# Busy matmuls in a TensorE gap and an earlier last gather, at the layer ends of a DMA-bound decode kernel

## The chip, the cores and the metric

One core of one Trainium2 chip. The metric is the device time of one execution in microseconds (us); the spread between executions of one kernel here is 1 to 3 us of some 1985. The core's engines are TensorE (matrix products), VectorE, ScalarE and SyncE (which issues the transfers here); DMA engines move the data from HBM, the chip's large memory, into the core.

## The reference

Four layers, A, B, A, B, each a residual attention block for one token over a cached context of 8192 positions, 32 heads of 192:

```python
# x: [1, 1, 640] bf16; k_cache, v_cache: [1, 32, 8192, 192]; wq: [640, 6144]; wo: [6144, 640]
def _A_ref(x, k_cache, v_cache, wq, wo):        # _B_ref is the same with its own arrays
    q = (x @ wq).reshape(B, Sq, Hq, Dh).transpose(0, 2, 1, 3)
    scores = jnp.einsum("bhqd,bhkd->bhqk", q, k) * (Dh ** -0.5)
    p = _softmax(scores, axis=-1)
    o = jnp.einsum("bhqk,bhkd->bhqd", p, v)
    return o.transpose(0, 2, 1, 3).reshape(B, Sq, Hq * Dh) @ wo
...
x = x + _A_ref(_layernorm(x), ...)              # then B, A, B
```

Every layer works on about 200 MB of K and V; with the weights, and less what two layers leave on the core for the later ones, 848 MB must come in from HBM. There is little arithmetic.

## The kernel before

Heads go in 16 pairs. Per pair, VectorE multiplies K by the query, TensorE sums the products through an identity matrix into the bank S, a softmax follows, TensorE multiplies the probabilities with V into the bank O ("values"), and a "gather" picks the right blocks out of O on VectorE (8 steps, 2 for the last pair) and moves them on with small matmuls into TB. After every 5 pairs "columns" turns the collected row into columns (`oT`), and "project" multiplies it with the 15 blocks of a part of wo, one matmul with one moving column per block and output group. The order of a layer's end is in a list of steps; every engine works the list in its order:

```python
# ... a part of the loop over layers l; p is the last pair, 15; NB = [0, 5, 0, 5]
steps.append(("e", l, p - 1))                                     # gather of pair 14
steps += [("v", l, p, 0), ("wc", l, 2)] if NB[l] else [("wc", l, 2), ("v", l, p, 0)]
steps += [("wo", l, 2), ("v", l, p, 1)]                           # wo: first 10 of 15 blocks
if NB[l]:
    plan.append(("vq", l))                                        # last quarter of pair 15's V
    both(("wob", l))                                              # the last NB[l] = 5 wo blocks
steps.append(("e", l, p))                                         # gather of pair 15
both(("wol", l))                                                  # pair 15's own rows of wo
```

`plan` is the order of these transfers, all issued by SyncE on one queue. At the end of a B layer it is: first half of pair 15's V, the third quarter, the last quarter (`vq`), the last five wo blocks (`wob`), pair 15's rows of wo (`wol`). `wol` lands in a row buffer, so its issue must wait for "columns" (`wc`); in layer 1 the first wq rows of layer 2 are issued right behind it.

## Time and profile before

| | before |
|---|---|
| time at first, 3 runs | 1984.95 us (1984.85 to 1985.31) |
| span of the profiled run, granted clock | 1984.0 us, 0.776 |
| DMA | 848.36 MB, 428 GB/s over the span |
| landing of `wob` in layer 3 | 1977.70 us |
| from there to the end of the last matmul | 3.29 us |
| from there to the end of the span | 6.3 us (2.4 of them the store of the result) |

The table's landings are in the trace's records of when each transfer's semaphore was updated: 16 updates, as many as the page counts DMA engines, and the transfer has landed with the last. The granted clock is the mean share of its full clock that TensorE was given; the trace's records of it hold 1.00 and 0.50 alone, in stretches that are multiples of 3.413 us (all 202 of the profile before but the last, in which the record ends). The lines of a profile's timeline in this document read: start, duration, engine, line of the kernel, operation, tiles (written <- read), shapes and count; in brackets the idle time before and what ended it. PE stands for TensorE's matmuls, DVE for VectorE, ACT for ScalarE. The lines of a chain of waits have the start, the duration and what was waited for. To read the table: the DMA stream fills the span (428 GB/s as a mean, 427 to 438 in 37 of its 40 slices), so there are two kinds of place where time can be won, at a stretch where the stream runs dry, and in the tail after its last landing.

### The profile page before, as it was taken

The numbers are of one execution on the slowest core, as the hardware profiler recorded it, in microseconds if no ns is written. First come the engines' busy times: TensorE is split into PE (matmuls) and PEld (weight loads), VectorE is DVE, ScalarE is ACT, GpSimd is POOL, SyncE is SP. The second block draws the span as 40 slices with busy tenths as digits, with TensorE's granted clock in tenths as the row PEclk, the third lists the DMA queues.
The fourth block names the chain that finished last, engine by engine and source line by source line (L and its number), as shares of the span: only waits on it lengthen the run. The fifth ranks groups of instructions, "written<-read, shape, count | busy, mean of one in ns | idle before, by whom it ended". The sixth has DMA issues, their size and how long they took to land.

```text
span 1984.0 us, 13908 instructions
## 1 busy us (share of the span) xinstructions
PE 1273.4 (64%) x8310; PEld 150.1 (8%) x3266; DVE 1200.7 (61%) x1371; ACT 139.5 (7%) x461; POOL 4.5 (0%) x22
## 2 busy tenths in 40 slices
PE   3567567566466666665775665675676766656657
PEld 0001001000200100100020010010002001001001
DVE  3566467467166656556745565665664775665665
ACT  0000000000000000000010000000000000000000
POOL 0000000000000000000000000000000000000000
PEclk9787777777587787777876777878886887777777
DMA  9999999999999999999999999999999999999998
GB/s 412 438 430 431 431 437 429 431 430 431 433 435 431 432 429 436 430 431 432 427 388 433 430 430 430 432 430 430 431 431 427 435 432 434 430 432 432 432 431 353
DMA packets 26926, 849.25 MB, mean 428 GB/s; under 512 B 3184, under 2 KB 3184, under 8 KB 3952
## 3 DMA queue, kind: packets, MB, share of 16 engines
q1 hardware_dynamic: 26720, 848.38, 99.5%
q8 instruction: 45, 0.74, 0.2%
q14 instruction: 17, 0.14, 0.0%
q10 hardware_dynamic: 144, 0.00, 0.0%
HBM read 848.36 MB, written 0.00 MB: 428 GB/s over the span
## 4 chain that ended last, share of the span: by engine, by line
DMA 68%; DVE 15%; PE 15%; ACT 1%; issue 0%; SPq 0%
DMA pool<-in_B_k_cache_dram 27%; DMA pool<-in_A_v_cache_dram 20%; DMA pool<-in_A_k_cache_dram 14%; DVE pool L543 13%; PE S L58 6%; PE OY L58 5%; DMA pool<-in_B_v_cache_dram 4%; PE OY L620 3%; DMA pool<-in_B_wo_dram 2%; ACT p_sb L580 1%; DVE acc L639 1%; DMA pool<-in_A_wq_dram 1%; DVE s_sb L565 1%; PE OY L513 0%; PE S L556 0%
## 5 line engine op out<-in xcount | busy, mean ns | idle before, releaser
L543 DVE TENSOR_TENSOR pool<-pool,q_sb 128x3072 bf16<-128x3072 bf16 x512 | 861.2, 1753 | 241.5 <-DMA pool<-in_B_k_cache_dram 144.0
L58 PE MATMUL S<-pool,ident 128*128 128x512 bf16 x2944 | 789.1, 425 | 20.3 <-DVE pool L543 19.0
L650 PE MATMUL TB<-acc,small 128*1 128x192 f32 x240 | 82.1, 493 | 219.1 <-DVE acc L639 219.1
L556 PE MATMUL S<-pool,ident 128*128 128x512 bf16 x128 | 62.9, 491 | 213.6 <-DVE pool L543 213.6
L58 PE MATMUL OY<-pool,p_sb 128*16 128x512 bf16 x1920 | 197.0, 485 | 0.0
L638 DVE TENSOR_SCALAR acc<-OY,small 128x192 f32<-128x192 f32 x64 | 26.7, 418 | 274.2 <-PE OY L58 246.2
L620 PE MATMUL OY<-pool,p_sb 128*16 128x512 bf16 (+1 forms) x1216 | 147.5, 497 | 62.7 <-DMA pool<-in_A_v_cache_dram 56.4
L639 DVE SCALAR_TENSOR_TENSOR acc<-OY,small,acc 128x192 f32<-128x192 f32 x424 | 177.1, 418 | 14.9
L565 DVE TENSOR_REDUCE s_sb<-S 128x64 f32<-128x512 f32 x128 | 88.1, 688 | 69.4 <-PE S L58 69.4
L502 ACT ACTIVATE q_sb<-QM 128x192 bf16<-128x192 f32 x60 | 19.9, 331 | 954.8 <-PE QM L496 954.8
L661 ACT ACTIVATE rows<-TB,small 1x192 bf16<-1x192 f32 x120 | 43.2, 406 | 585.1 <-PE TB L650 585.1
L634 DVE RECIPROCAL small<-TB 1x2 f32<-1x2 f32 x64 | 11.2, 175 | 96.7 <-PE TB L595 75.2
L580 ACT ACTIVATE p_sb<-s_sb,small 64x128 bf16<-64x128 f32 x128 | 55.7, 435 | 161.9 <-DVE small L574 161.1
L556 PEld LDWEIGHTS S<-pool,ident 128*128 128x128 bf16 x128 | 13.0, 101 | 686.2 <-DVE pool L543 636.4
L595 PE MATMUL TB<-small,ones 128*1 128x2 f32 x120 | 11.4, 165 | 74.1 <-ACT p_sb L580 74.1
L620 PEld LDWEIGHTS OY<-pool,p_sb 128*16 128x16 bf16 (+1 forms) x1216 | 39.3, 107 | 203.6 <-issue 133.5
L570 PE MATMUL QM<-ident,m_bf 128*64 128x64 bf16 x128 | 14.1, 217 | 54.4 <-DVE m_bf L567 53.8
L650 PEld LDWEIGHTS TB<-acc,small 128*1 128x1 f32 x240 | 19.7, 101 | 311.4 <-DVE acc L639 283.9
L513 PE MATMUL OY<-oT,pool 128*128 128x1 bf16 x900 | 38.2, 178 | 3.5 <-ACT oT L528 2.8
L513 PEld LDWEIGHTS OY<-oT,pool 128*128 128x128 bf16 x900 | 37.1, 131 | 7.0 <-ACT oT L528 3.6
L574 DVE TENSOR_REDUCE small<-QM 128x1 f32<-128x64 f32 x64 | 14.4, 225 | 36.1 <-PE QM L570 36.1
L496 PEld LDWEIGHTS QM<-rows,one_b 1*64 1x64 bf16 x120 | 6.2, 100 | 350.7 <-issue 344.8
(59 smaller groups left out, 186.1 us busy)
## 6 DMA issues: line engine op xcount, KB each, us to landing
pool<-in_B_k_cache_dram SPq DMA_DIRECT2D x28, 6144.0 KB, 38.1
pool<-in_B_v_cache_dram SPq DMA_DIRECT2D x28, 6144.0 KB, 34.2
pool<-in_A_v_cache_dram SPq DMA_DIRECT2D x27, 6144.0 KB, 27.6
pool<-in_A_k_cache_dram SPq DMA_DIRECT2D x34, 3072.0 KB, 20.4
pool<-in_A_k_cache_dram SPq DMA_DIRECT2D x14, 6144.0 KB, 36.8
pool<-in_A_v_cache_dram SPq DMA_DIRECT2D x10, 3072.0 KB, 14.3
pool<-in_B_k_cache_dram SPq DMA_DIRECT2D x8, 3072.0 KB, 22.7
pool<-in_A_wo_dram SPq DMA_DIRECT2D x6, 2400.0 KB, 21.4
```

The source lines that it names most:

```text
L58: return t.add_instruction(mybir.InstMatmult(name=t.bass.get_next_instruction_name(), engine=mybir.EngineType.PE, ins=[t.lower_ap(rhs), t. ...
L502: lambda a: a.activation(q_sb[i][:], QM[:, 0:DH], ACT.Copy), e, last["q"][i], bank=QMu)
L513: e = PE.op(lambda t, i=i, c=c, f=y_first[0], fin=n[0] == "wol" and i == k - 1: t.matmul(YB[:, c:c + 1], lhsT=t3[:, i, c:D:DC], rhs=o[:, i ...
L543: e = DV.op(lambda v, d0=d0: v.tensor_tensor(k3[:, :, d0:d0 + QD], kin[:, :, d0:d0 + QD], q_sb[qi][:, d0:d0 + QD].unsqueeze(1).broadcast_t ...
L556: t.matmul(S[:, :], lhsT=ident[:], rhs=k3[:, :, d0:d0 + R], start=True, stop=fin) if d0 == 0 else
L565: lambda v, u=u: v.tensor_reduce(s[:, u * JU:(u + 1) * JU], SP_[u][:].rearrange("p (j r) -> p j r", r=R), AX.X, ALU.add), ev_S[p, u], last ...
L580: ev_p[p] = AC.op(lambda a, h=h, r=r: a.activation(p_sb[par][r, :, h], s[r, :], ACT.Exp, bias=negm[par][r, 0:1], accum_out=l_col[par][r, h ...
L620: t.matmul(o, lhsT=x, rhs=y, start=f, stop=fin) if c == 0 else
L638: v.tensor_scalar(acc[:], O[:, 0:DH], pick[:, 0:1], None, ALU.mult) if i == 0 else
L639: v.scalar_tensor_tensor(out=acc[:], in0=O[:, i * DH:(i + 1) * DH], scalar=pick[:, i:i + 1], in1=acc[:], op0=ALU.mult, op1=ALU.add)), e if ...
L650: e = PE.op(lambda t, h=h: t.matmul(TB[96:97, C_O + h * DH:C_O + (h + 1) * DH], lhsT=half[:, h:h + 1], rhs=acc[:], start=True, stop=True), ...
L661: last["TO"] = last["row_written"] = AC.op(lambda a, h=h: a.activation(orow[:, o0 + h * DH:o0 + (h + 1) * DH], TB[96:97, C_O + h * DH:C_O ...
```

## The change

It is meant to do two things at the ends of layers 1 and 3 (the two B layers). While VectorE picks pair 14 out of the bank O, TensorE idles for 4.15 us, and its granted clock is 0.50 from 1966.99 on in layer 3 and from 1001.02 on in layer 1 (1.00 before); 16 matmuls of the identity on itself, written to a bank that nobody reads, are to keep it up. And the gather of pair 15 is put ahead of the last wo part, so that ScalarE's step behind the gather lies beside that part.

```diff
@@ -262,13 +262,15 @@
-            steps.append(("e", l, p - 1))
+            steps += [("busy", l, 16), ("e", l, p - 1)] if NB[l] else [("e", l, p - 1)]
             steps += [("v", l, p, 0), ("wc", l, 2)] if NB[l] else [("wc", l, 2), ("v", l, p, 0)]
             steps += [("wo", l, 2), ("v", l, p, 1)]
             if NB[l]:
                 plan.append(("vq", l))
+                steps.append(("e", l, p))
                 both(("wob", l))
-            steps.append(("e", l, p))
+            else:
+                steps.append(("e", l, p))
             both(("wol", l))
@@ -412,6 +414,16 @@
+        def busy(n):
+
+            PE.wait(ev_const, last["S"][0])
+            for i in range(n):
+                PE.op(lambda t, i=i: (
+                    t.matmul(SP_[0][:, :], lhsT=ident[:], rhs=ident[:].unsqueeze(1).broadcast_to([P, 4, P]), start=True, stop=True)
+                    if i == 0 else
+                    matmul_held(t, SP_[0][:, :], ident[:], ident[:].unsqueeze(1).broadcast_to([P, 4, P]), True, True)),
+                    signal=False, bank=Su[0])
@@ -672,6 +684,8 @@
+                elif n[0] == "busy":
+                    busy(n[2])
```

## The prediction

> **What bounds the kernel now.** I read the page first, for the engines and the DMA rows. They say that the sixteen DMA engines are never idle for long while TensorE and VectorE are busy some 60% each.
>
> ```profile
> PE 1273.4 (64%) x8310; PEld 150.1 (8%) x3266; DVE 1200.7 (61%) x1371; ACT 139.5 (7%) x461; POOL 4.5 (0%) x22
> ...
> DMA  9999999999999999999999999999999999999998
> GB/s 412 438 430 431 431 437 429 431 430 431 433 435 431 432 429 436 430 431 432 427 388 433 430 430 430 432 430 430 431 431 427 435 432 434 430 432 432 432 431 353
> ```
>
> The stream runs at some 430 GB/s everywhere but in slice 20 (from layer 1 into layer 2, 388) and in the last slice (353). 848.36 MB at 430 GB/s are 1973 us of the 1984, so all starts, ends and gaps together are worth about 11 us. The change touches just these two places, the ends of layers 1 and 3. So next I read the chain of waits there.
>
> ```profile
> 987.05 15.80 DMA pool<-in_B_v_cache_dram
> 1002.89 2.73 PE OY L620 x32
> ...
> 1007.03 13.21 DMA pool<-in_A_wq_dram
> ...
> 1937.57 40.13 DMA pool<-in_B_wo_dram
> 1977.74 1.16 PE OY L513 x25
> 1978.90 0.99 PE TB L646 x12
> 1980.23 0.77 PE OY L513 x15
> ```
>
> The reader is to see that the end of the kernel hangs on a transfer, the last part of wo, which lands at 1977.70; after it come 25 matmuls, the last pair's gather, and 15 matmuls. In layer 1 the chain goes through the first half of pair 15's values, then by the issue at 1007.03 to the landing of layer 2's first wq rows at 1020.24. Then the timeline of the last 25 us:
>
> ```profile
> 1962.13 0.22 PE L570 MATMUL QM<-ident,m_bf 128*64 128x64 bf16 x2
> ...
> 1963.31 3.14 DVE L639 SCALAR_TENSOR_TENSOR acc<-OY,small,acc 128x192 f32<-128x192 f32 x7
> ...
> 1966.50 0.99 PE L650 MATMUL TB<-acc,small 128*1 128x192 f32 x4 [4.15 <-DVE acc L639]
> ...
> 1968.70 2.73 PE L620 MATMUL OY<-pool,p_sb 128*4 128x384 bf16 x32
> ...
> 1977.59 0.42 DVE L638 TENSOR_SCALAR acc<-OY,small 128x192 f32<-128x192 f32 x1 [4.66 <-PE OY L620]
> ```
>
> TensorE idles 4.15 us while VectorE picks pair 14; the 32 value matmuls after it take 2.73 us, eight groups of four at 0.32 us, that is 384 columns at 1.2 per ns. The view by windows shows the clock as granted: 1.00 until 1967.0, 0.50 from there to the end. In layer 1 the gap is 4.15 us too and the clock 0.50 from 1001.0 to 1024.9.
>
> [...] the records of the clock hold only 1.00 and 0.50, in stretches of multiples of 3.413 us. I laid that grid over the trace. [...] The one-column matmuls of the wo part do not count: 0.86 of a window of them left it at 0.50. [...]
>
> **The change part by part.** (1) It adds 16 matmuls of 128x512 on the identity per B layer, 32 in all. At full clock, which the gap starts in at both places, one takes 0.216 us (12 value matmuls of 512 columns in four column groups take 0.65, so 0.217 a group), 16 take 3.46. They run from 1962.35 to 1965.8 (layer 3) and 995.99 to 999.45 (layer 1); the gather of pair 14 that follows needs TensorE at 1966.49 and 1000.14. So they fit in the gap with 0.7 us to spare and cost nothing.
>
> (2) What they buy. In layer 3, any window ending between 1965.8 and 1970.4 then holds at least 1.4 us of wide work (busy matmuls, gather 0.81, values), so the first half of the values of pair 15 should run at full clock: 8 groups of 0.163 and 0.15 of tail, 1.45 us instead of 2.73: 1.28 us saved, and 0.18 on the gather's matmuls (0.81, as in layer 1, for 0.99). In layer 1 the values start at 1002.89, bound by their landing, with 3.4 us since the last busy matmul; about a third of the positions of the window would lose the clock before them. When it holds, 1.28 us are saved there. After that come 3.2 us of one-column matmuls, which don't count, so by the second half of the values the clock is half again.
>
> (3) Where the gain goes. In layer 3 the second half of the values would start at 1973.35 instead of 1974.80, but its second quarter lands at 1975.77 (the trace's records of landings), and layer 1 shows 1.48 us from that restart to the end of the values at half clock (1010.25 to 1011.73). So they end at 1977.30 instead of 1977.53: 0.23 us of 1.46 are left. The pick on VectorE takes 0.06 + 0.87, to 1978.23.
>
> (4) The order. Before, from the landing of wo at 1977.70: wo 1.16, gather 1.04 overlapped by 0.07, ScalarE with its waits 0.36, wol 0.76: the last matmul ends at 1980.99. After, TensorE must wait for the pick: gather 1978.27 to 1979.31, wo 1.10 to 1980.41, wol 0.70 to 1981.1, with ScalarE beside wo. Hiding 0.36 costs an idle wait of 0.5. Sum: +0.1 us. If the values' second half ran at full clock, the pick would end 0.65 earlier and the sum would be about -0.5.
>
> (5) Layer 1: the same working, with the values' end unchanged at 1011.73, gives +0.1 us to the layer's end, which has slack: VectorE starts layer 2's products at 1018.57 while TensorE waits for wq until 1020.24. What could gain is the issue of that wq, 1.28 us earlier. The DMA rate had sunk to 232 and 247 GB/s at 1006 to 1008. But the landings say something else: 1006.54, 1010.20, 1012.14, 1013.32, 1020.24; their steps of 3.66, 1.94, 1.18 and 6.92 us are their bytes (1536, 800, 480, 2880 KB) at 430 GB/s. [...] So the landing at 1020.24 should hardly move: 0 to -0.6 us (the 0.6 if I am wrong and the mean rate counts: 1.28 us times 0.45 idle share).
>
> Total: +0.1 in layer 3, -0.3 in layer 1 as the middle of its two readings: -0.2 us, 1984.75. I lean a little further, to 1984.6, because the clock's phase can also help the second half of the values.
>
> **The rivals.** First: the warm clock carries through to the end, values, gather and wol all faster, and the order pays its full 0.36 + 1.04: about -1.5 us, with 0.6 of layer 1 some -2, 1983. For it: the whole tail from 1967.0 is at 0.50. Against it: the wo part between doesn't count, and transfers gate the tail. Second: the busy matmuls get in the way. Had the clock been at half there, they would take 6.8 us and hold the gather up by 2.7 us in each layer, of which the DMA backlog hides most: up to +3 us, 1988. Against it: dense work precedes the gap in both places and the clock is 1.00 there. Third: wo behind the gather frees its slot 1.5 us later in layer 1, and the wq rows for that slot are issued at 1014.9 instead of 1013.4; [...] I expect 0, at worst +0.5.
>
> **Range and chances.** The three runs of before spread 0.46 us. With the free window phase I take -1.4 to +1.0 around 1984.9 as the eight in ten: 1983.5 to 1985.9. Two per cent are 40 us, more than all gaps together on the fast side; only an accident could reach it: 1% on either side.
>
> **What would show it.** Right: 32 more S matmuls of 0.22 us; the idle time before L650 down from 4.15 to 0.7 us in layer 3; the first half of pair 15's values at 1.45 us, the second at 2.7 or stretched by its landing; L646 ahead of the 25 wo matmuls; the wo part's landing still some 6 us before the end, with the tail after it within 0.3 us of before. Wrong: a granted clock of 1.00 at the last values, or layer 2's first wq landing more than 0.6 us earlier, would mean a gain over 1 us; busy matmuls of 0.43 us would mean a loss.

That 1.4 us of wide matmuls in a window keep the clock up, in (2), and with it the third of the window's positions that would lose it, were the author's estimate. It came from two windows of the profile before: one with S matmuls for 1.26 us of its 3.41 (from 1673.45) was followed by a granted clock of 0.50, one with 1.39 (from 1731.47) by 1.00. That the one-column matmuls do not count is read from such windows too (2.95 us of them from 332.01 at 0.50, then 0.50 again). That nothing is won in (5) rests on the steps between the landings alone.

## The result

The change's median is 1985.45 us (1984.82 to 1987.35, 6 runs), that of the kernel before in the same rounds and the first ones 1985.51 us (1984.85 to 1986.53, 6 runs). The ratio is 1.0002 with a 95% interval of 0.9989 to 1.0015: the same. (A ratio here is the mean time of one kernel's fast runs over that of the other's, so it is not quite the ratio of the medians quoted.) A later trial of five rounds gave 0.9999. The time lies inside the forecast range, but that range of 2.4 us is about as wide as the runs scatter. The gain of 0.35 us against 1984.95 that was forecast did not show: the time came out 0.85 us above the forecast 1984.6, and 0.56 us of that is the kernel before itself, whose median went from 1984.95 to 1985.51 with three more runs. The interval is some 2.6 us to either side, so the times cannot tell a gain of 0.35 us from none; the traces must.

From the page of the profile after, the span, the busy time of the engines and the DMA rate by slices: 32 matmuls more, 8 us more of busy TensorE, the same two weak slices.

```profile
span 1983.5 us, 13942 instructions
...
PE 1281.3 (65%) x8342; PEld 149.7 (8%) x3268; DVE 1200.4 (61%) x1371; ACT 139.5 (7%) x461; POOL 4.4 (0%) x22
...
GB/s 412 435 434 429 430 435 432 432 429 430 434 432 436 430 429 432 432 434 430 424 402 438 425 430 430 432 431 430 433 431 428 434 430 434 431 434 433 430 432 350
```

The timeline of TensorE at the end of layer 3, after (lines lie 12 further down than before):

```profile
1961.92 0.39 PE L422 MATMUL S<-ident 128*128 128x512 bf16 x1
...
1962.14 3.40 PE L58 MATMUL S<-ident 128*128 128x512 bf16 x15
...
1966.13 0.81 PE L662 MATMUL TB<-acc,small 128*1 128x192 f32 x4 [0.59 <-DVE acc L651]
...
1968.06 1.47 PE L632 MATMUL OY<-pool,p_sb 128*4 128x384 bf16 x32
...
1972.90 1.45 PE L632 MATMUL OY<-pool,p_sb 128*4 128x384 bf16 x16
...
1974.82 1.45 PE L632 MATMUL OY<-pool,p_sb 128*4 128x384 bf16 x16 [0.46 <-DMA pool<-in_B_v_cache_dram]
```

The busy matmuls do what they were put in for: they fill the gap down to 0.59 us, the gather's matmuls take 0.81 instead of 0.99 us and the first half of pair 15's values 1.47 instead of 2.73. But the second half now stops in its middle for 0.46 us until the last quarter of its data has landed. Before, it ran through without a stop:

```profile
1974.80 2.73 PE L620 MATMUL OY<-pool,p_sb 128*4 128x384 bf16 x32
```

(Its quarter landed at 1975.77, and four groups of 0.32 us from 1974.80 on take until some 1976.1.) The view by windows of 3.413 us, the unit of the clock's records (stretch and its length; then busy time and count of PE, its weight loads, DVE, ACT and GpSimd; then the granted clock, the DMA share and rate), shows the clock that the second half got:

```profile
1965.30:1968.71 3.41, 1.92 (x27) 0.87 (x29) 0.74 (x2) 0.72 (x2) 0.00 (x0) 1.00 0.97 411
1968.71:1972.12 3.41, 3.13 (x71) 2.58 (x61) 0.17 (x1) 0.19 (x1) 0.00 (x0) 1.00 1.01 402
1972.12:1975.54 3.42, 2.96 (x50) 1.52 (x52) 0.00 (x0) 0.00 (x0) 0.00 (x0) 0.50 0.69 281
```

In the middle window TensorE is busy for 3.13 us of 3.41, but only 0.82 of that are values; the rest is columns and wo with one moving column each. The next window has 0.50, and the second half's groups take as long as before.

The chain of waits that ended last, after:

```profile
1937.51 37.26 DMA pool<-in_B_v_cache_dram
...
1974.82 1.48 PE OY L632 x15
...
1976.32 0.43 DVE acc L650
...
1976.78 0.43 DVE acc L651
...
1977.25 1.04 PE TB L658 x12
1978.29 1.71 PE OY L525 x40
```

Before, it hung on `wob`; now it hangs on the last quarter of V, landing at 1974.77, and goes through VectorE's pick and the gather into all 40 matmuls of the wo parts. `wob` itself lands at 1976.71, and TensorE waits for the pick until 1977.25. From that landing to the end of the last matmul (1979.98) are 3.27 us, against 3.29 before. That it is the last quarter that counts can be read across traces: in the five profiles of kernels that end layer 3 as the change does (the change twice, e5_delay6, e6_delay16, e7_warm2), the last matmul ends 5.21 us after that quarter's landing, while `wob` lands anything from 1.90 to 2.31 us after it. In this one profile everything is 1.0 us earlier by the landing of `wob`, but that is not the change: the change's second profile has it at 1978.02. 0.4 us of it are there before layer 2 begins, the other 0.6 come after; which part the phase of the clock's window has in that isn't shown.

In layer 1, the chain after reads:

```profile
1002.51 2.55 PE OY L632 x32
...
1006.46 13.40 DMA pool<-in_A_wq_dram
```

Here the granted clock of this execution fell to 0.50 at 1002.74, just after the values began, and they took 2.55 us. The first wq of layer 2 lands at 1019.85, 17.39 us after the first half of pair 15's V (1002.47); before it was 17.39 us too (1002.85 to 1020.24). The landing records show why the mean rate misleads here. The updates of one transfer have drifted apart: of the 16 of that first half of V, in the kernel before, the first came at 996.36 and the last at 1002.85, 6.5 us later (1.26 us in the first K transfer of layer 0). The updates that are ahead then have a gap, and the landing is the last one's: from `wob` to `wol` the first update takes 4.13 us (1005.70 to 1009.83), the last 1.18 (1012.14 to 1013.32), that is 480 KB at 417 GB/s.

### The profile page after: what moved, and what is told of

Its sections match the earlier page's. It is cut to its first block, busy times and chain, and to the rows that moved or that the text cites. A ratio compares the mean times of both kernels' runs of the same rounds, so it can differ in the third digit from the quotient of the medians.

```text
span 1983.5 us, 13942 instructions
## 1 busy us (share of the span) xinstructions
PE 1281.3 (65%) x8342; PEld 149.7 (8%) x3268; DVE 1200.4 (61%) x1371; ACT 139.5 (7%) x461; POOL 4.4 (0%) x22
## 4 chain that ended last, share of the span: by engine, by line
DMA 67%; PE 17%; DVE 14%; ACT 1%; issue 0%; SPq 0%
DMA pool<-in_B_k_cache_dram 27%; DMA pool<-in_A_v_cache_dram 20%; DMA pool<-in_A_k_cache_dram 14%; DVE pool L555 12%; PE S L58 8%; DMA pool<-in_B_v_cache_dram 5%; PE OY L58 5%; PE OY L632 3%; DVE acc L651 1%; ACT p_sb L592 1%; DMA pool<-in_A_wq_dram 1%; DVE s_sb L577 1%; PE S L568 0%; DVE m_bf L579 0%; PE OY L525 0%
```

## The experiments

Theory: the change's two gains are real and both are absorbed. The faster first half of the values is absorbed by the landing of the last quarter of V, the ScalarE time that the new order hides is absorbed by the wait for the pick, and in layer 1 the earlier issue of wq is absorbed because the last of a transfer's 16 updates, which is its landing, has no gap to lose. Rivals: the warm clock is worth its 1.3 us and the new order gives it back; the busy matmuls are worth nothing anywhere; the DMA stream's mean idle share in layer 1 counts, so that an earlier issue wins. The measure for layer 3 is the time from the landing of `wob` to the end of the last matmul, the "tail". (From there to the landing of the result, the 13 profiles have anything from 2.64 to 3.33 us, which blurs the times further.) All kernels gave correct results.

### The busy matmuls alone (e1_busy_only)

```diff
                 plan.append(("vq", l))
-                steps.append(("e", l, p))
                 both(("wob", l))
-            else:
-                steps.append(("e", l, p))
+            steps.append(("e", l, p))
```

> The 16 busy matmuls alone, last pair's gather back behind the wo part. Measure: from the landing of the last part of wo to the end of the last matmul (3.29 us before, 3.27 after, in their profiles). Gated theory (the second half of pair 15's values waits for its last quarter of data, whatever the clock did before): first half of the values 1.45 us as after, values end about 0.25 us earlier against the landing, VectorE's pick done before wo's 25 matmuls are, so 3.25 to 3.30 us, nothing won. Rival (the warm clock is worth its 1.3 us and the new order gives it back): about 2.0 us, and a time lower by about 1.3 us. Time within 0.1% of before either way.

Time 1985.38 us (4 runs) against 1985.82 (7 runs), ratio 0.9996 (0.9981 to 1.0011). The timeline of TensorE:

```profile
1975.58 1.45 PE L630 MATMUL OY<-pool,p_sb 128*4 128x384 bf16 x16 [0.62 <-DMA pool<-in_B_v_cache_dram]
1977.52 1.16 PE L523 MATMUL OY<-oT,pool 128*128 128x1 bf16 x25 [0.49 <-DMA pool<-in_B_wo_dram]
1978.60 1.04 PE L656 MATMUL TB<-small,acc 128*64 128x1 f32 x12
1980.00 0.76 PE L523 MATMUL OY<-oTl,rows 128*128 128x1 bf16 x15 [0.36 <-ACT oTl L666]
```

The tail is 3.29 us, exactly that of before. What the clock won goes into two waits for DMA, 0.62 us for the last quarter of V and 0.49 for `wob` (0.21 before). The first rival had said 2.0; it falls.

### The order alone (e2_order_only)

```diff
-            steps += [("busy", l, 16), ("e", l, p - 1)] if NB[l] else [("e", l, p - 1)]
+            steps.append(("e", l, p - 1))
```

> Gather ahead of the wo part, no busy matmuls. Gated theory: the values end some 0.2 us before the landing of wo as in before, pick done 0.76 us after it, then gather 1.04, wo 1.10, wol 0.74 behind one another: 3.6 us from the landing to the last matmul, 0.3 more than before. Rival (the order is worth the 0.36 us of ScalarE that it hides, wherever it stands): 2.9 us. First half of the values at 2.73 us, clock at half. Time within 0.1% of before either way.

Time 1987.23 us (4 runs) against 1985.82, ratio 1.0007 (0.9992 to 1.0022). The tail is 3.35 us, 0.06 more than before and a quarter us less than expected:

```profile
1975.81 2.73 PE L632 MATMUL OY<-pool,p_sb 128*4 128x384 bf16 x32
1979.52 0.90 PE L658 MATMUL TB<-small,acc 128*64 128x1 f32 x12 [0.98 <-DVE acc L651]
```

TensorE idles 0.98 us for the pick, 0.76 of it after the landing of `wob` at 1978.76. Of the difference to the expected 3.6, 0.14 is put down to chance: the clock's records of this run show full clock from 0.25 us after that landing, and the gather took 0.90 us instead of 1.04. The rest is overlap between the three groups that I had left out. So the order alone wins nothing and, at the usual clock, costs about 0.2 us. Only with the busy matmuls (pick ready 0.23 us sooner against the landing) does it come out even.

### The gate moved: 9 blocks instead of 5 behind the values (e3_nb9, g2_nb9_again)

```diff
-    NB = [0, 5, 0, 5]
+    NB = [0, 9, 0, 9]
```

> The change, with 9 instead of 5 of the 15 wo blocks of the last part loaded after pair 15's values: the values' last quarter lands 3.45 instead of 1.93 us before the end of the stream. Gated theory: with the gate moved, TensorE's own chain sets the end of the values, 1.8 us before the landing of wo; gather nearly done when wo lands, then 45 matmuls 2.0 us and wol 0.74: 2.85 us from the landing to the last matmul, 0.4 less than after. Rival (the tail after the landing is what counts, data of the values gates nothing): 20 more matmuls after the landing, 0.86 us more, 4.1 us.

Time 1984.72 us (4 runs) against 1985.82, ratio 0.9994 (0.9979 to 1.0009). Tail 2.60 us, 0.67 less than the change; the rival's 4.1 falls:

```profile
1971.69 0.82 PE L632 MATMUL OY<-pool,p_sb 128*4 128x384 bf16 x16
1973.86 1.45 PE L632 MATMUL OY<-pool,p_sb 128*4 128x384 bf16 x16 [1.35 <-DMA pool<-in_B_v_cache_dram]
1976.29 1.04 PE L658 MATMUL TB<-small,acc 128*64 128x1 f32 x12 [0.98 <-DVE acc L651]
1977.28 1.96 PE L525 MATMUL OY<-oT,pool 128*128 128x1 bf16 x45
```

The pick and all but the last 0.1 us of the gather are done when `wob` lands at 1977.24, and 45 matmuls and 15 for `wol` are all that is left. It went 0.25 us better than expected. One part is that I had TensorE's own chain setting the end of the values 1.8 us before the landing, while they end 1.93 us before it: with 20 wo matmuls fewer ahead of them and the clock still full (0.82 us for a quarter of the values, not 1.45), TensorE is at the last quarter early and waits 1.35 us for it. The rest is overlap between the groups of matmuls again.

The same kernel in five rounds (g2_nb9_again):

> The change with 9 wo blocks behind the values, again: tail 2.6 us, 0.7 less than the change and than before; time 0.7 us lower than the run above, 0.03%.

1985.68 us against 1985.91, ratio 0.9997 (0.9984 to 1.0009), tail 2.61. The tail repeats to 0.01 us; the time, at 0.3 us under the change's, doesn't tell a difference of this size.

### The gate moved, without the busy matmuls (e4_nb9_no_busy)

The edits of the last two experiments together.

> As the one before without the busy matmuls. Gated theory: now nothing hides the cold first half of the values, so all of the 1.45 us comes through: values end 0.35 us before the landing, pick 0.58 after it, then gather 1.04, wo 1.95, wol 0.7: 4.3 us from the landing to the last matmul, 1.45 more than with them. If the busy matmuls are worth nothing even there: the same 2.85 as with them. Time within 0.15% of before.

Time 1986.81 us (4 runs) against 1985.82, ratio 1.0008 (0.9991 to 1.0025). Tail 3.51 us, in its one profile:

```profile
1973.73 2.73 PE L632 MATMUL OY<-pool,p_sb 128*4 128x384 bf16 x32
1977.44 1.05 PE L658 MATMUL TB<-small,acc 128*64 128x1 f32 x12 [0.98 <-DVE acc L651]
```

Nothing waits for data any more in the values, they run through in 2.73 us, and the gather begins only when `wob` lands (1977.47). Against e3_nb9 the busy matmuls are worth 3.51 - 2.60 = 0.91 us. I had expected 1.45, since I had not seen that e3_nb9 would still be stopped by its data. So the second rival falls as well: the same 16 matmuls are worth 0.9 us as soon as the landing isn't in the way, and 0.0 (e1_busy_only) while it is.

### The issue of layer 2's wq put off (e5_delay6, e6_delay16)

```diff
-            steps += [("v", l, p, 0), ("wc", l, 2)] if NB[l] else [("wc", l, 2), ("v", l, p, 0)]
+            steps += [("v", l, p, 0)] + [("busy", l, 6)] * (l == 1) + [("wc", l, 2)] if NB[l] else [("wc", l, 2), ("v", l, p, 0)]
```

(16 in place of 6 in the second.) Both are measured from the landing of the first half of pair 15's V in layer 1.

> The change, with 6 more busy matmuls in layer 1 between the first half of pair 15's values and the columns that release wol and layer 2's wq: at half clock 2.6 us, so the wq issue goes 2.6 us later than in the change (about 6.6 us after the landing of the first half of the values instead of 4.0). [...] the first wq still lands 17.4 us after it, as in the four traces so far (issue at 3.4 to 4.6 us). Mean-rate theory (the idle engines at that time cost what they idle): 2.6 us times an idle share of about 0.45, 1.2 us later, 18.6.

> The same with 16: at half clock 6.8 us [...], issue of wq at 8.5 to 10.8 us after the landing of the first half of the values. [...] wol and wq land later by the rest, 1.5 to 3.8 us, so 18.9 to 21.2 for the first wq. Mean-rate theory: 6.8 times 0.45 or more, 20.5 and up, and no threshold between this run and the one with 6.

| kernel | wq issued | wq landed |
|---|---|---|
| before | 4.18 | 17.39 |
| the change | 3.99 | 17.39 |
| e1_busy_only | 3.38 | 17.40 |
| e2_order_only | 4.58 | 17.44 |
| the change, again (g1_change_again, below) | 2.91 | 17.44 |
| e7_warm2 (below) | 3.00 | 17.47 |
| e5_delay6 | 5.71 | 17.43 |
| e6_delay16 | 8.10 | 19.70 |

(us after the landing of the first half of pair 15's V.) The chain of waits of e5_delay6:

```profile
1005.44 0.45 PE S L422
1005.89 1.08 PE S L58 x5
1006.97 1.02 PE TB L537 x15
...
1008.38 11.72 DMA pool<-in_A_wq_dram
```

The six went at 0.22 us each (the last five took 1.08 us), not at 0.43, so they put the issue off by 1.5 us against before, not by 2.6. Still it is 2.7 us later than in e7_warm2, and the landing is the same to 0.04 us. By the mean-rate rival those 2.7 us should show as 1.2 us; it falls. The kernels with 9 blocks, whose stream has 1.5 us more ahead of wq (640 KB at 430 GB/s), say the same: issued at 4.04 (e3_nb9) and at 6.18 (e4_nb9_no_busy), wq landed at 18.93 in both. With 16, all 16 updates of wol come within 0.27 us (3.49 in before), and wol lands 0.7 us later behind `wob` than in e5_delay6. The landing of wq moves 2.3 us, to 19.70, within the 18.9 to 21.2 that were expected. So an issue at 5.71 us costs nothing and one at 8.10 does; from where on it costs isn't shown. Of the 16 updates of wq, 15 had come by 18.14, and the last came 1.56 us behind them; a 16 KB packet of instructions (0.88 us) began 2.1 us before that landing. Whether it held the last one up, this one profile can't show. The single times, 1985.85 and 1988.07 us, agree (before: 1985.81).

### Busy matmuls at the start of layer 2 (e7_warm2), and both versions together (e8_nb9_warm2, g3_nb9_warm2_again)

```diff
             elif l == 2:
                 plan += [("wq", l, g) for g in range(3)]
-                steps.append(("wq", l, 0))
+                steps += [("busy", l, 5), ("wq", l, 0)]
```

In the six traces so far, the later the clock rises in layer 2 (3.4 to 5.5 us after the landing of wq), the later that layer's first V transfer is issued (8.7 to 9.8 us after it), and the stream has a hole there (35 GB/s from 1029 to 1030 us in the profile before). When the clock would rise with the busy matmuls was worked out from what no trace shows, and is cut.

> The change, with 5 busy matmuls at the start of layer 2, where TensorE idles 2.2 us for its first wq rows. Phase theory: in the six traces so far the first values transfer of layer 2 is issued 8.7 to 9.8 us after the landing of wq, the later the later the clock rises (3.4 to 5.5 us after it), half a us for each us, and the stream runs dry there. [...] issue at 6.8 to 8.5, landing at 17.7 to 18.3 after the landing of wq instead of 18.6 to 19.8: about 0.9 us won on average. Rival (the busy matmuls hold up the wq rows, or VectorE's products set the pace): issue no earlier than 8.7. Tail of layer 3 as in the change: 3.3 us from the landing of wo to the last matmul.

Time 1985.52 us (4 runs) against 1985.81 (9 runs), ratio 0.9997 (0.9983 to 1.0010). The issue came 8.24 us after wq landed, earlier than in any trace before, as the phase theory has it; but the landing came at 19.1 us, no earlier. Its wq rows landed late (10.98 us after the first instead of 10.36 as in before; 10.4 to 12.0 in all traces), and what held them up I can't say. That expectation missed on the landing. Three transfers on, it is 41.0 us after wq's landing; the ten profiles without busy matmuls at the start of layer 2 have 41.4 to 42.7.

> Both improvements on the change: 9 wo blocks behind the values, 6 busy matmuls at the start of layer 2 (TensorE idles 2.9 us there with 9 blocks). Tail 2.6 to 2.9 us after the landing of wo (3.27 in the change); first values of layer 2 land 17.7 to 18.3 us after wq. Time lower than before by 0.6 plus 0.9 us, about 1.5 us or 0.08%, at the edge of what five rounds can tell (runs of one kernel spread over 2 us).

(With NB = 9, and 6 busy matmuls.) Time 1984.17 us (1983.69 to 1984.77, 5 runs) against 1985.81 (1985.48 to 1986.94, 9 runs), ratio 0.9990 (0.9976 to 1.0004). Tail 2.61 us as expected; the landing in layer 2, at 19.7, missed again (issue at 8.12; in its second profile the issue is at 7.15 and the landing at 18.4, the earliest of all). Then the unaltered change and this version in five rounds each on one chip, together with g2_nb9_again:

> The change itself, unaltered, on one chip with the two versions below. From the tails: 3.3 us from the landing of wo to the last matmul, as before; so the same time as before within 0.05%.

> The version with 9 blocks and the busy matmuls in layer 2, again. Its first trial was 1.6 us under before; of that the tail explains 0.7, and layer 2's first transfers showed no gain in its trace. If the 6 busy matmuls of layer 2 are worth nothing: the same as the run above. If they are worth what was hoped: 0.9 us lower than it.

| five rounds, one chip | median us | range | ratio to before | tail us |
|---|---|---|---|---|
| before (9 runs) | 1985.91 | 1985.39 to 1987.40 | | |
| the change, again | 1985.95 | 1985.42 to 1987.11 | 0.9999 (0.9985 to 1.0013) | 3.28 |
| NB = 9, again | 1985.68 | 1984.41 to 1986.82 | 0.9997 (0.9984 to 1.0009) | 2.61 |
| NB = 9 and layer 2, again | 1984.18 | 1983.71 to 1985.06 | 0.9990 (0.9978 to 1.0003) | 2.61 |

The version with both beat the kernel before in both trials, and the change in the one in which that ran too: its ten runs (1983.69 to 1985.06) all lie below the 18 runs of before in those trials (1985.39 and up). It is 0.1%, and the intervals still touch 1. About 0.7 us of it is the tail. The other 1.0 us isn't accounted for by any trace. In layer 2 the busy matmuls bring the issue of the first V forward in all three profiles that have them, but not the landings: two transfers after the first V, these three are at 33.7 us after wq by the mean, the other ten at 33.8. One transfer on they are 0.5 us ahead (41.5 against 42.0), since that step takes 7.3 us in two of them and some 8.3 in most others; the last point of this document has what coincides with it.

## Why the prediction was right or wrong

**The bound, right.** The stream's tail and the crossing from layer 1 to layer 2 were named as the places that could matter, and nothing that was tried there moved the time by much more than 0.1%. Nothing was tried elsewhere.

**The busy matmuls, right.** Forecast 3.46 us with 0.7 to spare, measured 3.62 with 0.59. Forecast 1.45 us for the first half of the values and 0.81 for the gather's matmuls in layer 3, measured 1.47 and 0.81. In layer 1 about a third of the window's positions were to lose the clock, by estimate: 4 of the 10 profiles with these matmuls did (1.92 to 2.73 us for the first half), the other 6 took 1.47.

**Where the gain goes in layer 3, right.** Forecast: of 1.46 us, 0.23 are left at the end of the values. Measured against the landing of `wob`: the values end 0.45 us before it instead of 0.17 (before's pick begins 0.11 before it, the change's 0.39), so 0.28 us. The restart took 1.45 us where 1.48 was taken from layer 1. The experiment that moved the gate shows the mechanism: 0.0 us with the gate, 0.91 with it moved.

**The order, right in kind, 0.1 us off.** Forecast +0.1 us, measured 3.27 - 3.29 = -0.02. The wait for the pick measured 0.54 us after the landing of `wob` where 0.57 was forecast, and the three groups of matmuls behind it overlap a little more than worked out. The chance that the second half of the values would run at full clock was not met where it counts: in layer 3 of every profile with the busy matmuls and 5 blocks the last quarter of the values, behind its landing, took 1.45 us.

**Layer 1: wrong, and this is the step that failed.** The prediction worked out that the landings keep their steps at some 430 GB/s, and then, in its words, took "-0.3 in layer 1 as the middle of its two readings". There was no middle: wq lands at 17.39 to 17.47 us whatever the issue between 2.9 and 5.7 us, so the term is 0.0. The mean-rate reading, a saved us of issue times the idle share, is what was false. The second failed step is the lean, "a little further, to 1984.6", for the clock's phase. Full clock did reach into the third quarter of the values in layer 3 in three of the profiles of this ending (0.82 us in e5_delay6 and e7_warm2, 1.09 in g1_change_again, for 1.45), and it bought nothing: TensorE then waited 1.70, 1.62 and 1.33 us for the last quarter. Without the two, its own sum would have been 1985.05 on the 1984.95 of before, which is no change within the noise, and that was measured.

**The rivals.** The warm clock carried through to the end in neither profile of the change. No busy matmul ran at half clock in the gap: 15 of them took 3.40 us in every profile. The wq rows for `wob`'s slot were issued at 1014.46 (forecast 1014.9, before 1013.38) and landed 6.91 us behind the ones before, as in the kernel before: 0 us, as forecast.

## What to carry to other kernels

In a kernel that is bound by its stream, speed up an engine only where its data is already there: look for the landing behind each step that gets faster, and move the landing first (here 9 blocks instead of 5 behind the values), then the faster clock is worth something. An idle share of the DMA engines as a mean did not tell here when a transfer lands (232 GB/s from 1007 to 1008 us, the landings' steps at some 430 all the same); compare the steps between landings with their bytes; where they agreed here, no earlier issue helped. And when two readings of one place contradict each other, test which one the trace supports rather than take their middle.

## What else the traces show

- The clock, by windows of 3.413 us in the profile before, each with what came in the next one. At 1.00, S matmuls for 0.37 of the window (from 1673.45; TensorE busy 1.67 us in all): 0.50. S matmuls for 0.41 (from 1731.47; busy 1.81 us): 1.00. At 0.50, values (16 stationary columns) for 0.80 (from 1076.11; busy 2.71 us): 1.00. S matmuls for 0.76 (from 1359.42; busy 2.59 us): 0.50. At 0.50, matmuls with one moving column for 0.86 (2.95 us, from 332.01): 0.50. In the profile after, at 1.00, busy for 3.13 us, all but 0.82 of it with one moving column (from 1968.71): 0.50.
- Pairs of a weight load of 128 columns and a bf16 matmul with one moving column went at 43 ns each (50 in 2.16 us): the same at a clock of 0.50 (before, from 1006.91) as with 1.00 for the first 1.31 us of them (after, from 1970.81).
- In the profile before, at the end of layer 1, the first of a transfer's 16 updates came 6.5 us ahead of the last, and the rate fell to 232 GB/s between 1007 and 1008 us while the landings kept their steps at some 430 GB/s (3.66 us for 1536 KB, 6.92 for 2880).
- Packets of 16 KB on an instruction queue took 1.0 us here (1058.4 us in the profile before), and the landing next after it came 1.07 us late (8.37 us for a step of 7.30). Of the five other steps of that profile that are late by about 1 us (the hole in layer 2 apart), one has such a packet within it and four have one of 8 KB (0.3 us) on the other instruction queue; most of the 45 packets of 16 KB have no late step behind them. That is a coincidence in time, not shown to be the cause, and no run here tested it.
